# One activation table set with ln and exp, loaded by name, in the head of an S5 scan and MLP block

## The chip, the cores and the metric

The kernel runs on one core of a Trainium2 chip. The metric is the device time of one execution in microseconds (us). Before the change eight executions give a median of 165.45 us, from 165.26 to 919.03; all but the one of 919.03 lie between 165.26 and 165.62.

## The reference

The input x has 2048 rows of 448 features. Everything starts from a layer norm of x; a state space branch and an MLP branch read it, and the MLP branch norms it once more.

```python
xn = _layernorm(x)
# branch A: a complex diagonal recurrence over the 2048 rows
dt = exp(log_dt); Lam_bar = exp(dt * Lam)
B_bar = ((Lam_bar - 1) / Lam)[:, None] * Bmat
Bu = einsum("bld,pd->blp", xn, B_bar)
h_t = Lam_bar * h_{t-1} + Bu_t
s = 2 * einsum("blp,dp->bld", h, Cmat).real + xn * Dskip
# branch B: an MLP with 1792 hidden features
y = _layernorm(xn)
h = gelu(einsum("bsd,df->bsf", y, w1) + b1)
g = silu(einsum("bsf,fd->bsd", h, w2) + b2)
return x + s * g
```

## The kernel before

The 2048 rows are cut into four groups (`g`) of 512, each of two blocks (`b`) of 256 rows, and each block holds its even and odd rows apart (`par`, two halves of 128 rows on the partitions). The recurrence advances two rows at a time, so that a group has 256 steps (NK).

The kernel is written as a list of 603 tasks. Each names its engine, the keys it reads and writes, and one or more instructions. `emit` (L106) issues them in the order of a written-out list, `ORDER` (L146), and puts a semaphore wait ahead of an instruction where a key demands one; each engine works its own queue in that order. Some tasks have two forms, for VectorE or ScalarE, or for GpSimd or VectorE, and the list `SECOND` (L164) says which take the second. `ORDER` and `SECOND` come from a planner outside the file; the durations and priorities in the calls are what it was given, and the kernel itself doesn't use them.

The head of the program:

- `parameters` (L445): TensorE turns the parameter rows into columns; ScalarE copies them out of PSUM (L455, L456) and takes exp twice (L458, L466); GpSimd computes sines, cosines and the coefficients of B_bar and C on tiny tiles (L459 to L518).
- TensorE multiplies the identity by itself 28 times, and 8 times more after the parameters (L764).
- `first_norm` (L359) takes block 0 half by half: statistics (L366) and their aggregate (L367) on VectorE, 1/sqrt of the variance on ScalarE as ln (L368) and exp (L369), the scaling on VectorE (L371), four transposes on TensorE (L374), and the copy out of PSUM (L376). The last ln and exp there (L378) and two GpSimd operations (L380) give the scale of the first norm.
- Block 1 of group 0 is normed without ScalarE (L393 to L403, L416), and transposed by TensorE (L432, L438).

```python
kb.add("act", [lambda e, ...: e.activation(r1, var, ACT.Ln, scale=1.0 + LN_EPS, bias=eps[:, 1:2]),
               lambda e, ...: e.activation(r1, r1, ACT.Exp, scale=-0.5)], [f"mv0_{q}", "eps", "warm"], [f"r1{par}"],
       dur=0.5, lat=0.2, prio=4 * PINNED, chain=True, table="exp")
```

The program has no table loads written in it; they are put in when it is built, wherever the active set lacks the next function. L280 is an ln on one element early in ScalarE's queue.

Then the work on TensorE runs in one stream:

- `mm1_half` (L688): the first matmul of the MLP for group 0, one block at a time. Seven groups of eight matmuls for each block (L694), each into one of three pairs of PSUM banks, and a gelu out of PSUM (L701) by ScalarE for each. The first three groups read the first half of w1, the fourth both halves.
- `mm1` (L674): the same for a whole later group (L678, gelu L685).
- `mm2` (L705): the second matmul, 14 matmuls (L709), then the bias (L712), a tanh (L713) and the product (L714), which make silu.
- `bu` (L604): the input of the recurrence (L608), copied out by ScalarE (L612, L614); `ssm` (L622): rotations on VectorE (L625 to L629), the scans (L633), copies (L637, L638) and the rotation back into the states h_sb (L661 to L665).
- `ym` (L717): the output of the recurrence (L730, and L733 or L739), the product with the MLP's (L743), the residual (L745), and the store.
- `lb`, `cq`, `m0` (L567, L586, L594) build the weights of the recurrence from B and C: a scaling (L558 on ScalarE or L559 on VectorE), a multiply-add (L561), and products (L597). `tables` (L526) builds the rotation tables with ScalarE's sine (L545). `skips` (L519) builds diagonal matrices De and Do (L522 on ScalarE or L523 on VectorE).
- `ln_stats`, `ln_scale`, `ln_apply` (L348, L383, L409) norm a later group; the apply is L416 on VectorE or L417 on ScalarE. The transposes of normed rows (xnT, xn2T), of B (BT) and of C (Cr) go through SP's DMA queue (L83), as do nearly all loads (L84). The bias b2bc is loaded through GpSimd's queue.

Of the kernel before, what the change touches and what calls it, by code (L numbers as in the profile page):

```python
# [7 lines left out]
ACT = mybir.ActivationFunctionType  # L8
ALU = mybir.AluOpType
# [4 lines left out]
PINNED = -1e5  # L14
# [129 lines left out]


ORDER = [int(k) for k in """  # L146
11 13 18 22 12 10 0 19 23 1 9 20 24 5 81 21 25 16 17 14 27 2 3 6 26 15 83 28 4 84 29 89 8 36 85 30 38 90 86 82 91 7 31 87 39 92 41 32 40 42 88 46 95
93 43 33 47 45 94 48 34 96 97 106 57 98 44 108 49 107 99 100 35 101 55 110 50 56 109 51 112 111 37 141 102 114 113 103 138 144 104 136 52 177 134 58
142 116 115 60 59 61 105 143 53 118 179 65 150 54 117 165 62 120 151 63 119 163 64 148 69 137 122 149 66 121 152 67 146 124 68 155 123 70 71 153 126
76 156 125 77 75 154 128 79 166 127 80 73 157 130 140 72 145 74 299 78 147 132 129 298 131 272 303 300 178 133 304 301 181 305 302 139 306 135 158 164  # L150
268 273 167 180 169 159 168 160 170 182 280 173 161 307 183 310 316 308 317 174 309 313 311 229 269 171 312 314 276 172 230 185 175 162 176 184 231
270 186 274 271 358 277 232 318 275 278 281 233 279 282 315 359 283 360 188 234 237 187 235 361 238 362 190 236 239 189 246 364 363 247 191 243 319
242 193 365 366 194 195 245 320 196 368 197 402 367 406 403 321 407 404 369 408 405 370 409 322 240 410 241 248 323 244 371 199 200 257 372 324 203
251 411 252 414 253 412 254 417 204 255 256 198 420 258 325 259 373 415 260 376 261 418 326 201 416 202 215 421 216 380 205 219 377 220 378 206 249
384 379 413 223 217 224 374 227 250 207 385 218 386 462 375 208 387 221 228 209 463 222 225 464 226 210 381 263 382 466 465 383 262 211 467 264 468
328 212 265 192 266 470 327 267 469 329 213 471 336 333 472 214 509 513 506 474 510 473 334 337 284 508 475 512 507 511 335 514 476 285 286 330 331
338 287 477 347 515 518 348 349 332 519 480 350 351 288 340 341 342 289 343 516 290 344 339 345 346 291 481 478 353 482 479 517 488 292 293 520 483
352 294 354 489 484 355 490 356 419 295 357 491 296 422 554 485 297 521 388 522 524 555 486 423 389 525 390 487 391 424 425 392 393 395 426 427 396
397 398 428 523 432 429 399 558 526 430 400 431 394 433 556 401 559 438 437 527 557 434 435 442 562 528 436 451 439 444 452 529 453 441 454 563 455
440 560 443 445 446 447 448 449 530 566 450 456 561 457 531 567 458 459 564 532 460 461 536 533 565 535 492 537 534 544 568 545 493 494 540 538 495  # L160
539 542 546 572 496 548 543 497 541 499 573 547 569 570 576 550 574 500 498 571 501 549 580 551 552 553 502 575 581 577 582 587 503 578 583 504 584
579 505 588 589 591 585 586 590 595 592 593 599 596 594 597 600 598 601 602
""".split()]
SECOND = [int(k) for k in """  # L164
134 135 136 138 139 140 143 144 167 171 193 199 201 203 219 223 225 227 310 313 314 317 411 412 417 420 421 516 518 521 522 525
""".split()]


# [6 lines left out]
TWO_PI = 2.0 * math.pi  # L175


def bass_recurrent_scan__ssm_conv_s5__mixer_channel_mlp__prompt_kernel(
# [18 lines left out]
    with ExitStack() as es:  # L197
        def SB(name, shape, dtype=BF):
            return es.enter_context(nc.sbuf_tensor(name, shape, dtype))

        ident = SB("ident", [128, 128])
        mhalf = SB("mhalf", [128, 1, 1], F32)
        iota = SB("iota", [128, NK], F32)
        sgn = SB("sgn", [128, 4], F32)
# [54 lines left out]
        def pool(fn, reads=(), writes=(), dur=0.3, prio=0):  # L259
            kb.add("pool", fn, reads, writes, dur=dur, lat=0.15, prio=prio)  # L260

        def dve(fn, reads=(), writes=(), dur=0.2, prio=0):
            kb.add("dve", fn, reads, writes, dur=dur, lat=0.12, prio=prio)

        def act(fn, reads=(), writes=(), dur=0.6, prio=0, table=None):
            kb.add("act", fn, reads, writes, dur=dur, lat=0.2, prio=prio, table=table)

        def pe(fn, reads=(), writes=(), dur=0.2, prio=0):
            kb.add("pe", fn, reads, writes, dur=dur, lat=0.25, prio=prio)

        with nc.Block():

            S0 = -100
            pool(lambda e: e.memset(ident[:], 1.0), [], ["ident"], 0.2, S0)
            pool(lambda e: e.affine_select(ident[:], ident[:], [[1, 128]], ALU.is_equal, 0.0, base=0,
                                           channel_multiplier=-1), ["ident"], ["ident"], 0.4, S0)
            pool(lambda e: e.memset(sgn[:], -1.0), [], ["sgn"], 0.1, S0)
            pool(lambda e: e.affine_select(sgn[:, 0:1], sgn[:, 0:1], [[0, 1]], ALU.is_ge, 1.0, base=63,
                                           channel_multiplier=-1), ["sgn"], ["sgn"], 0.2, S0)
            act(lambda e: e.activation(sgn[0:1, 3:4], sgn[0:1, 2:3], ACT.Ln, scale=-1.0), ["sgn"], ["warm"], 0.2, 4 * PINNED, "exp")  # L280
            pool(lambda e: e.iota(iota[:], [[1, NK]], base=0, channel_multiplier=0,
                                  allow_small_or_imprecise_dtypes=True), [], ["iota"], 0.6, S0)

            pool(lambda e: e.tensor_scalar(sgn[:, 1:2], sgn[:, 0:1], -TWO_PI, None, op0=ALU.mult), ["sgn"], ["sgn1"], 0.2, S0)
            pool(lambda e: e.tensor_scalar(sgn[:, 2:3], sgn[:, 0:1], TWO_PI, None, op0=ALU.mult), ["sgn", "warm"], ["sgn2"], 0.2, S0)
            pool(lambda e: e.memset(sgn[:, 3:4], math.pi / 2), ["warm"], ["sgn3"], 0.1, S0)
            XN = ["xn0", "xn1"]
            XM = ["xm0", "xm1"]
            dve(lambda e: e.memset(vrows[:, 0:64], 0.0), [], ["vr"], 0.1, S0)
# [69 lines left out]
            def first_norm():  # L359

                for par in range(2):
                    q = 2 * par
                    var, mean = lnmv[:, 0, q, 1:2], lnmv[:, 0, q, 0:1]
                    r1 = lnw[:, 0, 2, 1, q:q + 1]
                    src, dst = x_all[:, 0, par, :], xn2_sb[:, 0, par * 512:par * 512 + D]
                    dve(lambda e, q=q, src=src: e.bn_stats(lnst[:, q, :], src), [f"x0p{par}"], [f"st{q}"], 0.62, 2 * PINNED + par)  # L366
                    dve(lambda e, q=q: e.bn_aggr(lnmv[:, 0, q, :], lnst[:, q, :]), [f"st{q}"], [f"mv0_{q}"], 0.16, 2 * PINNED + par)  # L367
                    kb.add("act", [lambda e, var=var, r1=r1: e.activation(r1, var, ACT.Ln, scale=1.0 + LN_EPS, bias=eps[:, 1:2]),  # L368
                                   lambda e, r1=r1: e.activation(r1, r1, ACT.Exp, scale=-0.5)], [f"mv0_{q}", "eps", "warm"], [f"r1{par}"],  # L369
                           dur=0.5, lat=0.2, prio=4 * PINNED, chain=True, table="exp")  # L370
                    dve(lambda e, src=src, dst=dst, mean=mean, r1=r1: e.tensor_scalar(dst, src, mean, r1, op0=ALU.subtract, op1=ALU.mult),  # L371
                        [f"x0p{par}", f"r1{par}", f"mv0_{q}", "xm0"], [f"xm0p{par}"], 0.4, 2 * PINNED + par + 0.5)
                    bank, oap = 6 - par, xn2T[:, 0, par * 4:par * 4 + 4, 0:128]
                    pe([lambda e, d=d, par=par, bank=bank: e.transpose(psh[:, bank, d * 128:(d + 1) * 128], xn2_sb[:, 0, par * 512 + d * 128:par * 512 + d * 128 + 128],  # L374
                                                                       ident[:, :]) for d in range(4)], [f"xm0p{par}", "ident"], [f"ps{bank}"], 0.33, 2 * PINNED)
                    dve(lambda e, bank=bank, oap=oap: e.tensor_copy(oap, psh[:, bank, 0:512].rearrange("p (d c) -> p d c", d=4)), [f"ps{bank}"], [f"xmT0p{par}"], 0.42, 2 * PINNED + 2)  # L376
                r0, n0, var = lnw[:, 0, 2, 0, 0:4:2], lnw[:, 0, 3, 0, 0:4:2], lnmv[:, 0, 0:4:2, 1]
                kb.add("act", [lambda e: e.activation(r0, var, ACT.Ln, bias=eps[:, 0:1]), lambda e: e.activation(r0, r0, ACT.Exp, scale=-0.5)],  # L378
                       ["mv0_0", "mv0_2", "eps", "r10", "r11"], ["r0"], dur=0.5, lat=0.2, prio=3 * PINNED, chain=True, table="exp")
                kb.add("pool", [lambda e: e.tensor_tensor(n0, lnmv[:, 0, 0:4:2, 0], r0, ALU.mult), lambda e: e.tensor_scalar(n0, n0, -1.0, None, op0=ALU.mult)],  # L380
                       ["mv0_0", "mv0_2", "r0"], ["lnw0_0"], dur=0.6, lat=0.15, prio=S0 + 2, chain=True)
# [467 lines left out]
```

## Time and profile before

| | |
|---|---|
| median of the runs | 165.45 us |
| the profiled execution's own time | 165.53 us |
| its span, from first to last instruction | 163.8 us |
| TensorE busy | 155.0 us, 95% of the span |
| VectorE busy | 124.6 us, 76% |
| ScalarE busy | 98.8 us, 60% |
| GpSimd busy | 33.8 us, 21% |
| mean granted clock of TensorE | 0.979 |
| chain that ended last, by engine | PE 91%, ACT 3%, DVE 2%, DMA 1%, issue 1% |

The profile is of one execution; its times are counted from the start of the span. PE is TensorE's matmul, PEld its weight load, DVE VectorE, ACT ScalarE, POOL GpSimd, and SP the engine that issues most transfers. A line such as L694 is a line of the kernel, and "a<-b" says what an operation writes and reads. The chain is followed back from the last instruction to whatever released it. A wait is written as the waiting operation, then the one that released it, then the total, the number and the longest.

### The profile page before, as it was taken

To read this page: it belongs to the slowest core of one execution; us is meant where nothing else is said; L and a number is where in the kernel's file an instruction comes from. 1 tells how busy PE (TensorE), PEld (TensorE's weight loads), DVE (VectorE), ACT (ScalarE), POOL (GpSimd) and SP (SyncE) were. 2 spreads that over 40 slices of the span, in tenths; PEclk is the share of its full clock that TensorE was granted. 3 is DMA by queue.
4 is the path that set the end of the run, shared out by engine and by line. 5 is a ranking of instruction groups with operands and counts; after the bars stand their busy time and mean duration, and the time that the engine had idled before them with its cause. 6 is when DMAs were issued, how large, how long until landed. Compare 5 with 4: busy or idle time off the path is not lost.

```text
span 163.8 us, 2747 instructions
## 1 busy us (share of the span) xinstructions
PE 155.0 (95%) x977; PEld 100.0 (61%) x977; DVE 124.6 (76%) x251; ACT 98.8 (60%) x156; POOL 33.8 (21%) x115
## 2 busy tenths in 40 slices
PE   5569999999999999999999999999999999999991
PEld 5448996567766765555555555566767675555560
DVE  5175698977498998899996969732499489987953
ACT  4998979987958599966544580452158953360200
POOL 5227795500000580000205420000002300000000
PEclk9956999999999999999999999999999999999999
DMA  4999946999874007300000056402060000010021
GB/s 100 332 284 382 255 58 139 185 161 179 164 147 116 0 0 133 107 0 4 0 0 0 2 123 122 112 0 56 4 168 0 0 4 0 0 56 0 35 83 58
DMA packets 29880, 14.61 MB, mean 89 GB/s; under 512 B 24581, under 2 KB 29577, under 8 KB 29866
## 3 DMA queue, kind: packets, MB, share of 16 engines
q1 hardware_dynamic: 29810, 14.31, 36.6%
q0 software_dynamic: 48, 0.11, 0.6%
q8 instruction: 8, 0.13, 0.3%
q14 instruction: 6, 0.05, 0.1%
q10 hardware_dynamic: 8, 0.00, 0.0%
HBM read 6.77 MB, written 1.84 MB: 53 GB/s over the span
## 4 chain that ended last, share of the span: by engine, by line
PE 91%; ACT 3%; DVE 2%; DMA 1%; issue 1%; DVEq 0%
PE psum L709 26%; PE psum L678 22%; PE psum L608 13%; PE psum L730 12%; PE psum L694 9%; PE psum L733 4%; PE psum L597 3%; ACT L369 2%; DMA x_all<-in_A_x_dram 1%; PE psum L739 1%; DVE t L743 1%; ACT L368 1%; DVE tmp L745 1%; DVE lnst L366 0%; PE psum L374 0%
## 5 line engine op out<-in xcount | busy, mean ns | idle before, releaser
L709 PE MATMUL psum<-w_sb,gT 128*128 128x448 bf16 x224 | 44.2, 352 | 0.0
L678 PE MATMUL psum<-xn2T,w_sb 128*128 128x512 bf16 x168 | 38.6, 379 | 0.0
L709 PEld LDWEIGHTS psum<-w_sb,gT 128*128 128x128 bf16 x224 | 21.8, 98 | 19.3
L685 ACT ACTIVATE gT<-psum 128x1024 bf16<-128x1024 f32 x21 | 21.5, 1024 | 14.9 <-PE psum L678 12.9
L678 PEld LDWEIGHTS psum<-xn2T,w_sb 128*128 128x128 bf16 x168 | 21.6, 132 | 12.5 <-issue 0.2
L608 PE MATMUL psum<-xnT,BT 128*128 128x256 bf16 x196 | 24.0, 273 | 0.0
L608 PEld LDWEIGHTS psum<-xnT,BT 128*128 128x128 bf16 x196 | 19.0, 98 | 4.7 <-ACT u_sb L612 0.3
L743 DVE TENSOR_TENSOR t<-psum,g_sb 128x448 bf16<-128x448 f32 (+2 forms) x17 | 10.1, 595 | 10.5 <-PE psum L733 8.5
L713 ACT ACTIVATE th<-o 128x448 f32<-128x448 f32 x16 | 8.8, 571 | 12.0 <-DVE o L712 11.9
L694 PE MATMUL psum<-xn2T,w_sb 128*128 128x256 bf16 x112 | 14.8, 301 | 0.6 <-issue 0.6
L633 DVE TENSOR_TENSOR_SCAN s_f<-cw,cur,v_sb 128x256 f32<-128x256 f32 x21 | 14.7, 736 | 0.3
L694 PEld LDWEIGHTS psum<-xn2T,w_sb 128*128 128x128 bf16 x112 | 13.2, 136 | 2.1 <-issue 0.8
L612 ACT ACTIVATE u_sb<-psum 128x512 bf16<-128x512 f32 x12 | 7.1, 595 | 10.0 <-PE psum L608 9.4
L712 DVE TENSOR_TENSOR o<-psum,b2bc 128x448 f32<-128x448 f32 x16 | 9.8, 622 | 4.4 <-PE psum L709 4.1
L730 PE MATMUL psum<-CQ,h_sb 128*128 128x448 bf16 (+2 forms) x63 | 12.0, 332 | 0.0
L730 PE MATMUL psum<-CZ,h_sb 128*128 128x448 bf16 x56 | 11.9, 352 | 0.0
L417 ACT ACTIVATE xn_sb<-x_all,lnw 128x448 bf16<-128x448 bf16 x16 | 11.4, 749 | 0.1
L714 DVE SCALAR_TENSOR_TENSOR g_sb<-th,o 128x448 bf16<-128x448 f32 x16 | 9.8, 619 | 1.9 <-ACT th L713 1.8
L701 ACT ACTIVATE gT<-psum 128x512 bf16<-128x512 f32 x14 | 8.2, 592 | 1.7 <-PE psum L694 1.5
L730 PEld LDWEIGHTS psum<-CQ,h_sb 128*128 128x128 bf16 x63 | 6.0, 98 | 4.2
L352 DVE BATCH_NORM_STATS2 lnst<-x_all 128x6 f32<-128x448 bf16 x14 | 8.3, 603 | 0.0
L730 PEld LDWEIGHTS psum<-CZ,h_sb 128*128 128x128 bf16 x56 | 5.4, 98 | 4.6
(151 smaller groups left out, 197.4 us busy)
## 6 DMA issues: line engine op xcount, KB each, us to landing
w_sb<-in_B_w_dram SPq DMA_DIRECT2D x2, 784.0 KB, 9.3
out_dram<-tmp SPq DMA_DIRECT2D x7, 224.0 KB, 2.2
w_sb<-in_B_w_dram SPq DMA_DIRECT2D x2, 672.0 KB, 6.2
x_all<-in_A_x_dram SPq DMA_DIRECT2D x3, 448.0 KB, 3.8
gT<-in_A_C_re_dram SPq DMA_DIRECT2D x1, 392.0 KB, 12.0
Bn<-in_A_B_re_dram SPq DMA_DIRECT2D x1, 336.0 KB, 8.2
Bn<-in_A_B_im_dram SPq DMA_DIRECT2D x1, 336.0 KB, 8.2
gT<-in_A_C_im_dram SPq DMA_DIRECT2D x1, 336.0 KB, 3.9
```

The costliest lines, as they stand in the source:

```text
L417: ("act", lambda e: e.activation(dst, src, ACT.Identity, bias=nb, scale=rs), 0.75, 0.2)]
L608: fns = [lambda e, r=r, m=m, d=d: e.matmul(psum[:, 4, r * NK:(r + 1) * NK], BT[:, m, d, :], xnT[:, gx, d, :], start=(d == 0), stop=(d == 6 ...
L633: dve(lambda e, i=i, ri=ri, init=init: e.tensor_tensor_scan(s_f[:, i, ri, :], col(R2, i).to_broadcast([128, NK]), v_sb[:, i, ri, :], init, ...
L678: fns = [lambda e, k=k, d=d: e.matmul(psum[:, b0 + k, :], w1_sb[:, d, fcol(2 * j + k)], rhs[:, d, :, :], start=(d == 0), stop=(d == 3)) fo ...
L685: act(lambda e: e.activation(gT[:, gb, 2 * j:2 * j + 2, :], psum[:, b0:b0 + 2, :], ACT.Gelu_apprx_tanh), [f"ps{b0}", f"ps{b0 + 1}"] + (WK ...
L694: fns = [lambda e, k=k, d=d: e.matmul(psum[:, banks[k], :].rearrange("p (r c) -> p r c", r=2)[:, :, cs], w1_sb[:, d, fcol(2 * j + k)], rhs ...
L709: fns = [lambda e, fi=fi: e.matmul(psum[:, bk, 0:D], gT[:, gb, fi, q * 128:(q + 1) * 128], w2_sb[:, fi, :], start=(fi == 0), stop=(fi == N ...
L712: dve(lambda e: e.tensor_tensor(o2[:, fb, :], psum[:, bk, 0:D], b2bc[:], ALU.add), [f"ps{bk}", "b2bc"], [f"oo{fb}"], 0.62, prio - 76)
L713: act(lambda e: e.activation(th[:, fb, :], o2[:, fb, :], ACT.Tanh, scale=0.5), [f"oo{fb}"] + (WK + WKP if g == 0 else []), [f"th{fb}"], 0. ...
L714: dve(lambda e: e.scalar_tensor_tensor(out=g_sb[:, gs, :], in0=th[:, fb, :], scalar=1.0, in1=o2[:, fb, :], op0=ALU.add, op1=ALU.mult), [f" ...
L730: fns = [lambda e, k=k: e.matmul(psum[:, bk, c0:c1], h_sb[:, hb, k, k0:k0 + 128], cm[:, k, c0:c1], start=(k == 0), stop=False) for k in ra ...
L743: dve(lambda e: e.tensor_tensor(t3[:, fb, c0:c1], psum[:, bk, c0:c1], g_sb[:, gs, c0:c1], ALU.mult), [f"ps{bk}", f"g{gs}"], [f"t3{fb}_{c0} ...
```

## The change

The activation of L280 is replaced by a load, by name, of the table set `natural_log_exp_and_others`, which waits for nothing. The keys that kept two small GpSimd operations (L285, L286) behind it go. The identity's two GpSimd operations get another priority. `ORDER` and `SECOND` are replaced whole.

```diff
 ORDER = [int(k) for k in """
-11 13 18 22 12 10 0 19 23 1 9 20 24 5 81 21 25 16 17 14 27 2 3 6 26 15 83 28 4 84 29 89 8 36 85 30 38 90 86 82 91 7 31 87 39 92 41 32 40 42 88 46 95
...
+0 11 18 22 12 1 10 19 23 13 9 81 20 24 2 14 3 21 16 25 6 7 27 17 15 5 26 83 8 28 4 84 29 89 38 85 30 90 82 86 91 31 87 39 92 32 41 40 42 88 46 95 93
...
 SECOND = [int(k) for k in """
-134 135 136 138 139 140 143 144 167 171 193 199 201 203 219 223 225 227 310 313 314 317 411 412 417 420 421 516 518 521 522 525
+135 137 138 142 143 163 165 167 173 175 201 203 215 221 223 225 227 310 313 411 414 418 420 421 515 516 522 524
...
-            pool(lambda e: e.memset(ident[:], 1.0), [], ["ident"], 0.2, S0)
+            pool(lambda e: e.memset(ident[:], 1.0), [], ["ident"], 0.2, 3 * PINNED)
             pool(lambda e: e.affine_select(ident[:], ident[:], [[1, 128]], ALU.is_equal, 0.0, base=0,
-                                           channel_multiplier=-1), ["ident"], ["ident"], 0.4, S0)
+                                           channel_multiplier=-1), ["ident"], ["ident"], 0.4, 3 * PINNED)
...
-            act(lambda e: e.activation(sgn[0:1, 3:4], sgn[0:1, 2:3], ACT.Ln, scale=-1.0), ["sgn"], ["warm"], 0.2, 4 * PINNED, "exp")
+            act(lambda e: e.preload_act_table_set("natural_log_exp_and_others"), [], ["warm"], 0.05, 5 * PINNED, "exp")
...
-            pool(lambda e: e.tensor_scalar(sgn[:, 2:3], sgn[:, 0:1], TWO_PI, None, op0=ALU.mult), ["sgn", "warm"], ["sgn2"], 0.2, S0)
-            pool(lambda e: e.memset(sgn[:, 3:4], math.pi / 2), ["warm"], ["sgn3"], 0.1, S0)
+            pool(lambda e: e.tensor_scalar(sgn[:, 2:3], sgn[:, 0:1], TWO_PI, None, op0=ALU.mult), ["sgn"], ["sgn2"], 0.2, S0)
+            pool(lambda e: e.memset(sgn[:, 3:4], math.pi / 2), ["sgn"], ["sgn3"], 0.1, S0)
...
-                           dur=0.5, lat=0.2, prio=4 * PINNED, chain=True, table="exp")
+                           dur=0.55, lat=0.2, prio=4 * PINNED, chain=True, table="exp")
```

What the new lists do on each engine's queue:

- GpSimd makes the identity ahead of the memset of M0 (L293), which was first. The load of b2bc, which stood behind L286, stands behind some 40 operations of the parameters.
- ScalarE's activations keep their order up to the second gelu. Later, among the tasks with two forms, it has 5 more of L558, 3 more of L522 and 3 fewer of L417; VectorE has 5 fewer of L559, 3 fewer of L523 and 3 more of L416.
- VectorE's first 23 rows (up to the apply of block 1 of group 0) are the same. Ahead of the last step of group 0's states (L665) it now has four statistics of group 3 (L352, L356), which stood behind it.
- TensorE's order is the same up to the first `mm2`. Then the group-1 `mm1` begins with two groups of eight and not one; the group-2 `mm1` begins ahead of the first `m0` and not behind it; the first `ym` comes behind five groups of group 2's `mm1` and not seven; one group of group 3's `mm1` goes earlier. The matmuls themselves are the same.
- SP's queue has the same loads up to x of group 1. Then C_im's larger piece is ahead of C_re, its last piece and two of the BT transposes are behind the transposes of group 1's xn2T and the first of its xnT, and later transposes of a group stand ahead of some of the stores.

## Prediction

> **What bounds the kernel now.** I read the waits of TensorE first, then the chain that ended last in order of time, then the stretches of TensorE's clock, then the landings of the loads. TensorE waits three times, and never after 10.39 us; from there to 158.6 us the chain is TensorE alone.
>
> ```profile
> PE psum L374 <- DVE xn_sb L371: 2.7, 1, 2.7
> PE psum L764 <- POOL ident L275: 1.8, 1, 1.8
> PE psum L694 <- issue: 0.6, 1, 0.6
> ```
>
> So the kernel is a head of 10.39 us, then 148.2 us of matmuls in a row, then 5.2 us of tail. The head is this part of the chain (start, length, what):
>
> ```profile
> 3.79 0.29 ACT lnw L368
> ...
> 4.11 1.28 ACT L369
> ...
> 5.40 0.20 ACT lnw L369
> ...
> 5.62 1.28 ACT L368
> ...
> 7.23 1.28 ACT L369
> 8.51 0.01 issue
> 8.52 0.21 ACT lnw L369
> 8.73 0.03 issue
> 8.76 0.41 DVE xn_sb L371
> 9.17 0.05 issue
> 9.21 0.61 PE psum L374 x4
> 9.82 0.56 issue
> 10.39 6.82 PE psum L694 x40
> ```
>
> The nameless ACT pieces of 1.28 us are table loads: the ln and the exp of each half of block 0 evict each other, and three loads lie between the first variance and the second half's scale. The first 40 matmuls take 6.82 us where the next 72 take 7.86 us, because of the clock (columns: stretch, its length, TensorE's busy time, and after POOL the granted clock):
>
> ```profile
> 4.85:8.27 3.42, 1.58 (x23) 1.08 (x21) 0.40 (x1) 3.36 (x5) 0.27 (x2) 1.00 1.02 320
> 8.27:11.68 3.41, 1.90 (x11) 1.33 (x12) 2.52 (x7) 3.32 (x8) 1.18 (x5) 0.50 1.03 273
> 11.68:15.10 3.42, 3.42 (x18) 2.47 (x17) 2.47 (x13) 3.21 (x7) 2.36 (x11) 0.50 1.07 365
> 15.10:18.50 3.40, 3.40 (x37) 3.39 (x36) 1.17 (x6) 2.96 (x6) 2.56 (x11) 1.00 1.06 359
> ```
>
> A stretch that is 46% busy is followed by half clock, one of 56% leaves it there, a full one lifts it. One limit lies just behind the head: the last piece of w1's second half, issued at 4.20 us, lands 7.7 us later, at 11.9.
>
> ```profile
> L84 SPq DMA_DIRECT2D w_sb<-in_B_w_dram x1: 497/497/497, 4.2 to 4.2; - x1
> ...
> DMA to landing us min/median/max: 7.7/7.7/7.7
> ```
>
> **What the skill says.** "ScalarE: Activation LUTs", Table sets: one named set, natural_log_exp_and_others, holds both functions; no run here shows that yet. The same page, What ACT_TABLE_LOAD costs: 1283 ns a load, equal for every set, and some 1380 ns of drain. The trace agrees on 1.28 us; the gaps around a load in the chain are 0.02 us, so I price a load at 1.3. "TensorE: Matmul & The Clock Gate", What's actually happening: the clock is decided in free-running windows of 3413 ns. The trace agrees: 8.27, 11.68 and 15.10 are 3.41 apart.
>
> **The change, part by part.** *Loads.* The order of the built program has one load ahead of the eight ln and exp activations instead of six, the other four (L701, L545, L713, L685) stay: 5 x 1.28 = 6.4 us less on ScalarE, plus the 0.20 us of L280's activation. What counts is the part ahead of TensorE. The one load now stands behind the ACT DMA issues (2.13 us) and ends at about 3.45, before the first variance at 3.77. Then ln and exp of half 0: 3.79 to 4.30. Half 1's variance ends at 4.30 + 0.18 = 4.48; its ln and exp (0.29 + 0.20) at 5.01; its L371 at 5.43 instead of 9.17. TensorE's four transposes of half 0 end at 6.49 as before (warm-up matmuls stand ahead), those of half 1 follow at once, to 6.8; the two copies L376 (0.42 each) run 6.53 to 7.37; matmuls follow 0.11 later, as before (10.28 to 10.39): 7.5. GpSimd now makes the identity before its 0.47 us memset, so TensorE's first warm-up moves 0.4 earlier and this may be 7.1; w1's first half, last piece issued at 2.18, lands 4.9 later, at 7.1, so not sooner.
>
> *What is late next.* Three groups of eight matmuls need only w1's first half; the fourth needs the second: 11.9. At full clock a matmul takes 7.86/72 = 0.11 us, at half 0.22. If the clock stays full, 24 take 2.6 and end near 10.1: TensorE stands for 1.8. If it drops at 8.27, seven are done by then and 17 x 0.22 = 3.7 end at 12.0. Either way group four begins at 12.0. Before: 22 matmuls by 15.10, two more by 15.3. Gain 15.3 - 12.0 = 3.3 us, not the 3.84 of three loads and not the 2.9 by which the start moves.
>
> *The clock after 12.0.* Not shown by the trace, bounded both ways. Stretch 4.85 to 8.27 will be some 70% busy (1.58, plus 0.77 to 1.1 of new matmuls), between 46 (dropped) and the 88 of the stretch before 4.85 (the warm-ups from 1.83 on, 0.11 us each; the eight after it take 0.08, so the clock was lifted). If it drops at 8.27 the next stretch is full and the clock is back at 11.68: cost nothing. If it stays, the next stretch is half busy; if that again suffices, cost nothing; if it drops at 11.68, then 14 matmuls run at half clock up to 15.10: 14 x 0.11 = 1.55 us. Two of three paths are free; I take nothing, range 0 to 1.55.
>
> *Evacuation.* The gelu load now ends near 8.0, before group one (8.4 at the soonest). 14 groups cost 0.59 each, and 2 L417 (0.75), 4 L522 (0.39), 2 L558 (0.65) go among them: 8.3 + 1.5 + 1.6 + 1.3 = 12.7 between 8.4 and 22.2; three pairs of banks give slack. Hidden; without that cover each L417 would cost 0.75.
>
> *b2bc.* Its DMA moves on GpSimd behind some 40 small operations, to about 18; at 7.3 us from issue to landing (as before, under more traffic) 25.3. Its first reader L712 comes at 24.9, the bank is wanted at 27.5: hidden, 0 to 0.4. Its 112 KB leave the first 12 us, which may bring w1 up to 0.4 us sooner.
>
> *The new order.* The matmuls are the same, so each wait is the question. I walked TensorE's new order with the old lengths (8 of L678 1.73, 14 of L608 1.53, 14 of L709 2.65, L730 1.32, L733 0.76), 3.3 ahead, and set against it when each operand is ready. Moved to DVE: 3 more L416 (0.39); moved to ScalarE: 5 L559 (0.45) and 3 L523 (0.25), so DVE loses 1.8 us net. Thin places: xn2T of group 1, wanted at 35.9; its last apply stands behind the sine table (load, five L545, one L417, to 30.2), the transpose goes out at 30.8 and takes 3.5 to 4.1: 34.9, slack 1.0. xn2T of group 2, now first used at 66.2 instead of 70.9: applies end at 61.3, lands 65.5, slack 0.7. States of group 0 (L665): ym now stands behind five mm1 groups of group 2, not seven: wanted at 87.33 - 3.3 - 2 x 1.73 = 80.6; DVE puts four more statistics (4 x 0.77) ahead of L665, but fewer L714 and L559; I get 78.2, slack 2.4. On SP's queue C_im's last piece and two BT transposes now go behind xn2T and xnT of group 1: the piece out at 34.7, landed 3.9 later at the latest, Cr's transposes (1.3 each) from 39.0 to 44.2, where they were 42.7 to 47.9; BT5 lands at 38.4, wanted at 39.4. I book 0.3 for all of it, range 0 to 2.
>
> *Sum.* Against the profiled execution: 165.53 (span 163.8, 1.73 around it) - 3.3 + 0.3 = 162.5; the median is 0.08 lower: 162.4.
>
> **Rivals.** (A) As above, 162.4. (B) The clock drops at 11.68 and takes back 1.55; TensorE is then later than its operands, so the 0.3 goes: 163.7. For it: 46 and 56% did not earn full clock. Against: two other paths. (C) The thin places give: 1 to 2 us of waits over A's, 163.9. For it: DVE is busy 34.5 of 37 us between 50 and 87. (D) Slower: the states of group 0 come late. If DVE gains nothing from the early head (it hangs on the Cr transposes) and pays all four statistics, L665 ends at 79.66 + 3.1 = 82.8; TensorE stands 2.2 of 3.41 us at L730, a stretch 35% busy, less than the 46% that cost the clock at 8.27, and a window at half clock adds 1.7: 162.1 + 3.9 = 166.0. It decides from L665 at about 82.6. Against: those transposes do come forward on SP's queue, and DVE has 1.8 less to do. (E) The set is not what it says, and loads come back: 165.5; the program's order has none.
>
> **Numbers.** A 0.50, B 0.27, C 0.13, D 0.07, E 0.03. Low end: w1 0.4 sooner and no wait, 161.7. High end: B with 0.6 of waits, 164.3. 0.2%, about what a measurement of this kernel can tell from no change, is 0.33 us: faster 0.90, same 0.03, slower 0.07.
>
> **What would show it.** One load at L280 and none at L368, L369, L378; L694 starting at 7.1 to 7.5; its 25th matmul at 12.0, behind w1; full clock from 11.68 (A) or 15.10 (B); no wait of TensorE over 0.5 us after 12. Wrong: a wait at L678 near 36 or 66, or at L730 near 80.

## The result, and the profile after

| | before | after |
|---|---|---|
| median of all runs | 165.44 us (31 runs) | 164.99 us (11 runs, 161.94 to 165.93) |
| the profiled execution: its time, its span | 165.53, 163.8 | 163.0, 161.3 |
| first L694, first L709, first L678 in the chain | 10.39, 25.52, 39.17 | 7.12, 20.40, 36.41 |

The ratio after to before is 0.9846, 95% interval 0.9821 to 0.9871, some 162.9 us; it leaves out runs more than 1.5% above the fastest of their kernel, and of the changed kernel's own eleven timed runs that is more than half, since they spread over 4 us where those of before lie within 0.9 (but for one at 919.03). So the change is a gain, about as large as forecast, that most executions don't get in full.

The profile of the changed kernel has one load ahead of ln and exp, and none between them (ScalarE's timeline; start, length, line and operation, and in brackets the idle time ahead and what ended it):

```profile
2.16 1.28 ACT L280 ACT_TABLE_LOAD   x1 [2.16 <-issue]
3.81 0.29 ACT L368 ACTIVATE lnw<-lnmv,eps 128x1 f32<-128x1 f32 x1 [0.37 <-DVE lnmv L367]
4.14 0.20 ACT L369 ACTIVATE lnw<-lnw 128x1 f32<-128x1 f32 x1
4.81 0.29 ACT L368 ACTIVATE lnw<-lnmv,eps 128x1 f32<-128x1 f32 x1 [0.46 <-DVE lnmv L367]
5.13 0.20 ACT L369 ACTIVATE lnw<-lnw 128x1 f32<-128x1 f32 x1
```

Before, 1.28 us of load stood between each pair; the named set does hold both functions, as the prediction took it. The waits of TensorE (the waiting operation, what released it, total, number, longest):

```profile
PE psum L678 <- DMA xn2T<-xn_sb: 1.4, 1, 1.4
PE psum L764 <- POOL ident L275: 1.4, 1, 1.4
PE psum L709 <- DVE o L712: 0.8, 1, 0.8
PE psum L694 <- DVE xn2T L376: 0.7, 1, 0.7
PE psum L694 <- issue: 0.2, 1, 0.2
```

The wait of 2.7 us at L374 is gone. Two are new and lie where TensorE never waited before: 0.8 us at L709 and 1.4 us at L678. The chain in order of time shows where:

```profile
7.12 2.80 PE psum L694 x24
9.92 0.24 issue
10.16 1.93 PE psum L694 x16
...
20.40 5.31 PE psum L709 x28
25.71 0.62 DVE o L712
26.33 0.14 issue
26.47 2.81 PE psum L709 x14
...
32.97 3.40 DMA xn2T<-xn_sb
36.37 0.05 issue
36.41 3.66 PE psum L678 x16
```

The first L709 comes 25.52 - 20.40 = 5.1 us earlier. From there to the first L678 it took 39.17 - 25.52 = 13.65 us before and takes 36.41 - 20.40 = 16.01 now: 2.36 us are given back, 0.8 and 1.4 of them in the two waits. After that little moves: 119.44 us from the first L678 to the last matmul's end before (158.61), 119.71 now (156.12). 5.12 - 2.36 - 0.27 = 2.49 us is the gain of this execution.

Two facts lie behind those numbers. The last piece of w1's second half, issued at 4.2 us as before, lands 5.9 us later, at 10.07, where it was 7.7 us. The fourth group of L694 starts there, at 10.16, though the profile names no releaser for it ("issue"):

```profile
L84 SPq DMA_DIRECT2D w_sb<-in_B_w_dram x2: 425/461/497, 3.7 to 4.2; - x2
...
DMA to landing us min/median/max: 5.8/5.8/5.9
```

And b2bc, whose turn on GpSimd came at 18.0, was issued at 21.91, after 3.9 us in which GpSimd did nothing (GpSimd's timeline):

```profile
17.79 0.22 POOL L490 TENSOR_SCALAR cw<-cw 128x4 f32<-128x4 f32 x1
21.91 0.80 POOL L84 DMA_DIRECT2D b2bc<-in_B_b_dram  x1 [3.91 <-issue]
```

It landed 3.8 us later, at 25.7, and there L712 starts (VectorE's timeline):

```profile
22.87 0.25 DVE L356 BATCH_NORM_AGGREGATE lnmv<-lnst 128x2 f32<-128x6 f32 x2
25.70 0.62 DVE L712 TENSOR_TENSOR o<-psum,b2bc 128x448 f32<-128x448 f32 x1 [2.58 <-PE psum L709]
```

The bracket names the matmuls, but the 14 that L712 needs were done by 23.05 (20.40 and 14 x 0.19): the one that came last was the load. Behind L712 in VectorE's queue stand the multiply-adds L561; the BT transposes on SP's queue wait for those, and xn2T of group 1 stands behind five BT transposes (SP's timeline):

```profile
21.07 10.50 SPq L83 DMA_TRANSPOSE BT<-Bn  x5
31.61 2.68 SPq L83 DMA_TRANSPOSE xn2T<-xn_sb  x2
```

### The profile page after: what moved, and what is told of

It reads as the page before. It is cut to its first block, busy times and chain, and to the rows that moved or that the text cites. A ratio compares the mean times of both kernels' runs of the same rounds, so it can differ in the third digit from the quotient of the medians.

```text
span 161.3 us, 2734 instructions
## 1 busy us (share of the span) xinstructions
PE 153.0 (95%) x977; PEld 99.0 (61%) x977; DVE 123.4 (77%) x246; ACT 95.0 (59%) x155; POOL 37.1 (23%) x115
## 4 chain that ended last, share of the span: by engine, by line
PE 91%; DVE 2%; DMA 2%; ACT 1%; issue 1%; POOL 0%; DVEq 0%; ACTq 0%; POOLq 0%
PE psum L709 25%; PE psum L678 23%; PE psum L608 12%; PE psum L730 12%; PE psum L694 8%; PE psum L733 4%; PE psum L597 3%; PE psum L764 2%; DMA xn2T<-xn_sb 2%; ACT tmp L558 1%; PE psum L739 1%; DVE t L743 1%; DVE tmp L745 1%; DVE xn2T L376 0%; DVE o L712 0%
## 5 line engine op out<-in xcount | busy, mean ns | idle before, releaser
L709 PE MATMUL psum<-w_sb,gT 128*128 128x448 bf16 x224 | 44.5, 352 | 0.8 <-DVE o L712 0.8
L678 PE MATMUL psum<-xn2T,w_sb 128*128 128x512 bf16 x168 | 39.1, 380 | 1.4 <-DMA xn2T<-xn_sb 1.4
L709 PEld LDWEIGHTS psum<-w_sb,gT 128*128 128x128 bf16 x224 | 21.7, 98 | 20.1 <-ACT WT L545 1.2
L678 PEld LDWEIGHTS psum<-xn2T,w_sb 128*128 128x128 bf16 x168 | 21.5, 132 | 14.1 <-DMA xn2T<-xn_sb 1.7
L712 DVE TENSOR_TENSOR o<-psum,b2bc 128x448 f32<-128x448 f32 x16 | 9.9, 622 | 6.8 <-PE psum L709 6.5
L694 PE MATMUL psum<-xn2T,w_sb 128*128 128x256 bf16 x112 | 12.8, 273 | 0.9 <-DVE xn2T L376 0.7
L694 PEld LDWEIGHTS psum<-xn2T,w_sb 128*128 128x128 bf16 x112 | 12.1, 132 | 1.3 <-DVE xn2T L376 0.9
L730 PE MATMUL psum<-CQ,h_sb 128*128 128x448 bf16 (+2 forms) x63 | 12.0, 332 | 0.0
L730 PE MATMUL psum<-CZ,h_sb 128*128 128x448 bf16 x56 | 11.9, 352 | 0.0
L417 ACT ACTIVATE xn_sb<-x_all,lnw 128x448 bf16<-128x448 bf16 x13 | 9.8, 753 | 2.1 <-DVE xn_sb L416 1.9
L701 ACT ACTIVATE gT<-psum 128x512 bf16<-128x512 f32 x14 | 8.2, 593 | 2.1 <-PE psum L694 1.8
L352 DVE BATCH_NORM_STATS2 lnst<-x_all 128x6 f32<-128x448 bf16 x14 | 8.3, 610 | 0.8 <-DMA x_all<-in_A_x_dram 0.8
L730 PEld LDWEIGHTS psum<-CQ,h_sb 128*128 128x128 bf16 x63 | 6.0, 98 | 4.4
L393 POOL TENSOR_SCALAR lnw<-lnmv 128x4 f32<-128x4 f32 x3 | 1.1, 380 | 32.1 <-DVE lnmv L356 32.0
```

Of the source, the lines that this page charges most:

```text
L417: ("act", lambda e: e.activation(dst, src, ACT.Identity, bias=nb, scale=rs), 0.75, 0.2)]
L678: fns = [lambda e, k=k, d=d: e.matmul(psum[:, b0 + k, :], w1_sb[:, d, fcol(2 * j + k)], rhs[:, d, :, :], start=(d == 0), stop=(d == 3)) fo ...
L694: fns = [lambda e, k=k, d=d: e.matmul(psum[:, banks[k], :].rearrange("p (r c) -> p r c", r=2)[:, :, cs], w1_sb[:, d, fcol(2 * j + k)], rhs ...
L709: fns = [lambda e, fi=fi: e.matmul(psum[:, bk, 0:D], gT[:, gb, fi, q * 128:(q + 1) * 128], w2_sb[:, fi, :], start=(fi == 0), stop=(fi == N ...
L712: dve(lambda e: e.tensor_tensor(o2[:, fb, :], psum[:, bk, 0:D], b2bc[:], ALU.add), [f"ps{bk}", "b2bc"], [f"oo{fb}"], 0.62, prio - 76)
L730: fns = [lambda e, k=k: e.matmul(psum[:, bk, c0:c1], h_sb[:, hb, k, k0:k0 + 128], cm[:, k, c0:c1], start=(k == 0), stop=False) for k in ra ...
```

## The experiments

My theory after the two traces: the loads are a gain of some 5 us because b2bc's traffic, gone from the first 12 us, lets w1 come sooner; 2.5 us of it are lost since b2bc comes too late at its new place. The rivals: the new order as a whole brings (or costs) the difference; or the spread is the clock's, and b2bc has no part in it. All ratios are against the kernel before. "Landing" below is that of w1's last piece after its issue at 4.2.

**b2bc through SP's queue.** The changed kernel with

```diff
-ld("pool", b2bc[:], dram_ap(B_b2, 0, [[0, 128], [1, D]]), ["b2bc"], 114688, -50, reads=["sgn3"])
+ld("sp", b2bc[:], dram_ap(B_b2, 0, [[0, 128], [1, D]]), ["b2bc"], 114688, -50)
...
+ORDER.remove(36); ORDER.insert(ORDER.index(37), 36)
```

> The changed kernel, with b2bc loaded through SP's queue just ahead of the load of x blocks 2 and 3, and not through GpSimd. Theory (GpSimd stood 3.9 us before it issued this load, so b2bc came 2.6 us late for L712, and what follows on VectorE and SP came late with it): L712 starts within 0.2 us of the end of its first 14 L709 matmuls (23.1), the TensorE waits of 0.8 us at L709 and 1.4 us at L678 go, and the time is 163.0 - 2.2 = 160.8 us, with runs that lie within 1 us of each other. Rival 1 (b2bc was not what L712 waited for, or x blocks 2 and 3 and the C matrices come later by as much): both waits stay within 0.5 us, 162.5 to 163.5. Rival 2 (the runs of the changed kernel at 165 us are another matter than b2bc): the profile is at 161, but the median stays above 163.5.

Measured: 162.14 us (161.41 to 163.56, 5 runs), 0.9789 (0.9768 to 0.9811). Below the changed kernel's interval, and rival 2 falls; but the theory's 160.8, with runs within 1 us, didn't come either. The profiled execution was this kernel's slowest, at 163.56, no faster than that of the changed kernel. The wait at L709 is gone there, but TensorE stood twice for w1 (its second half landed at 11.50), and 1.1 us at L678 stay, because this time x of blocks 2 and 3 was late (a wait of TensorE, then VectorE's timeline):

```profile
PE psum L694 <- DMA w_sb<-in_B_w_dram: 2.6, 2, 1.7
...
22.23 1.16 DVE L352 BATCH_NORM_STATS2 lnst<-x_all 128x6 f32<-128x448 bf16 x2 [2.15 <-DMA x_all<-in_A_x_dram]
```

They were there at 19.4 in the trace of the changed kernel. So L678 hangs on two things: the BT transposes ahead of xn2T, and x of blocks 2 and 3 behind w1, Bn, w2 and now b2bc on one queue.

**b2bc back at its early place on GpSimd**, the rest as changed:

```diff
+ORDER.remove(36); ORDER.insert(ORDER.index(8) + 1, 36)
```

> The changed kernel, with b2bc's load still on GpSimd but at its place of before, behind the memset L286, and so some 15 us earlier. Theory (the same as for b2bc on SP, and b2bc's early traffic is what kept w1's second half until 11.9 before): no wait at L712, no wait of 0.8 and 1.4 us, but w1's second half lands at 11.5 to 11.9 in place of 10.1, L694's 25th matmul goes then, and the time is 160.8 + 1.5 = 162.3 us. Rival (w1 came sooner for another reason, the earlier issue of loads on SP): w1 stays at 10.1 and the time is 160.8. If GpSimd's standing was not the cause of the late L712, it is 163 or above.

Measured: 164.66 us (163.12 to 167.04, 22 runs), 0.9916 (0.9895 to 0.9936). The waits at L709 and L678 went (0.2 left at L678), and w1 came late, more than expected: landing 9.3 us, at 13.5, with 3.1 us of TensorE standing ahead of it. By the ratios the early load costs more than the late one (0.9916 against 0.9846); the medians of all runs, 164.66 and 164.99, don't show it.

**The set alone.** The kernel before, in its own order:

```diff
-act(lambda e: e.activation(sgn[0:1, 3:4], sgn[0:1, 2:3], ACT.Ln, scale=-1.0), ["sgn"], ["warm"], 0.2, 4 * PINNED, "exp")
+act(lambda e: e.preload_act_table_set("natural_log_exp_and_others"), [], ["warm"], 0.05, 5 * PINNED, "exp")
```

with the two "warm" keys of L285 and L286 gone, as in the change.

> The kernel before in its own order, with nothing but the named set at L280 (and the two semaphore keys that go with it): one load in place of six. If the sum of the prediction holds for this part alone, L694 starts at 7.1 to 7.5, its 25th matmul waits for w1's second half at 11.5 to 12.0, and the time is 165.5 - 3.3 = 162.2 us with the full clock from 11.68. If the clock is lost in the window to 11.68, it is 163.7. If w1 comes sooner without the moved b2bc too, it is 161. If the loads were hidden, it is 165.4.

Measured: 164.0 us (163.09 to 166.64, 6 runs), 0.9893 (0.9871 to 0.9916). Nearer to 163.7 than to 162.2, for a reason that I had not put into any number: w1 came at 13.3, later than before (11.9), with b2bc issued at 3.5, ahead of both pieces of w1's second half (3.7 and 4.2), and not at 4.1 between them. In the profiled execution, one of the longer ones at 165.60, TensorE's waits have this line:

```profile
PE psum L694 <- DMA w_sb<-in_B_w_dram: 2.9, 1, 2.9
```

and the windows (columns as in the prediction) are these:

```profile
8.27:11.68 3.41, 2.23 (x21) 1.99 (x19) 1.47 (x5) 2.30 (x5) 2.37 (x11) 1.00 1.02 305
11.68:15.10 3.42, 1.68 (x8) 1.28 (x9) 3.04 (x16) 0.00 (x0) 2.59 (x13) 0.74 1.06 325
15.10:20.00 4.90, 4.90 (x43) 4.47 (x42) 2.87 (x9) 3.92 (x7) 3.36 (x16) 0.83 1.02 318
```

A w1 as late as this costs twice, here and in the trace with b2bc back at its early place: TensorE stands, and then goes on at half clock for a window, from 13.3 on here and from 13.1 there.

**The order alone.** The changed kernel with `preload_act_table_set("natural_log")` at L280, so that five loads come back.

> The changed kernel's order with six loads as before: L280 loads the set of ln alone, so that each exp and ln behind it loads its own again. If the loads and not the order bring the gain, L694 starts at 8.7 to 9.2, and b2bc's lateness costs as in the changed kernel: 163.0 + 1.6 = 164.6 us, or 166 and more if the clock drops in the window to 11.68 as before. If the new order brings most of the gain (w1 sooner at 10.1 in place of 11.9): 163.0 to 163.5.

Measured: 165.66 us (165.29 to 171.46, 22 runs), 1.0009 (1.0000 to 1.0019). No gain; L694 started at 10.49, not at 8.7 to 9.2, and b2bc's lateness costs nothing where everything else is late as well (issued at 23.8, after 0.55 us of standing, and read at 28.1).

**The set and b2bc on SP, in the old order**: the two edits above together, on the kernel before.

> The kernel before in its own order, with the named set at L280 and with b2bc loaded through SP's queue just ahead of the load of x blocks 2 and 3. Theory (the early b2bc load on GpSimd keeps w1's second half back: 11.3 to 13.4 us with it, 10.1 to 11.3 without it, in the five traces so far): w1's second half lands at 10.5 to 11.5 where it was 13.0 with the set alone, no lost clock, and the time is 164.0 - 2.0 = 162.0 us. Rival 1 (the new order is what gives the gain beside the loads): 163.5 to 164. Rival 2 (w1's landing is chance alone, whatever b2bc does): the runs spread from 163 to 166.6 as with the set alone.

Measured: 161.22 us (160.95 to 162.67, 6 runs), 0.9759 (0.9730 to 0.9788). All that the changed kernel was to bring, and without its order. w1 landed after 6.5 us, at 10.7; TensorE's waits are those of the head:

```profile
PE psum L764 <- POOL ident L275: 1.8, 1, 1.8
PE psum L694 <- ACT gT L701: 0.7, 1, 0.7
PE psum L694 <- DVE xn2T L376: 0.6, 1, 0.6
```

The second line names a gelu that the fourth group doesn't need: that group takes the first pair of banks again, and the gelu on that pair had ended at 8.97. What came last was w1, at 10.70, as the weight loads of the same matmuls say (TensorE's weight loads):

```profile
10.74 1.39 PEld L694 LDWEIGHTS psum<-xn2T,w_sb 128*128 128x128 bf16 x13 [0.91 <-DMA w_sb<-in_B_w_dram]
```

**C_im's larger piece late again**, on top of b2bc on SP in the new order (C_im's 336 KB behind the second BT transpose, its 56 KB piece in their early place):

```diff
+i, j = ORDER.index(178), ORDER.index(179); ORDER[i], ORDER[j] = 179, 178; ORDER.remove(178); ORDER.insert(ORDER.index(180) + 1, 178)
```

> The changed kernel with b2bc on SP, and with C_im's 336 KB piece put back to a late place on SP (behind the second BT transpose), its 56 KB piece in its stead, as the order before had it. Theory (C_im's 336 KB, moved into the early stretch by the new order, share the DMA engines with x blocks 2 and 3, whose landing at 22.2 in the trace with b2bc on SP set the end through xn2T): x blocks 2 and 3 land 1 us sooner or more, the wait of 1.1 us at L678 falls to 0.3 or less, and the time is 162.1 - 0.8 = 161.3 us. Rival (C's piece stands behind x in the queue and takes nothing from it): the same as with b2bc on SP, 162.1. If the later place holds up the BT transposes: 162.6 to 163.

Measured: 162.01 us (160.95 to 164.46, 6 runs), 0.9774 (0.9742 to 0.9807): the same as with b2bc on SP alone. x of blocks 2 and 3 came at 20.5 in this trace and at 22.2 in that, as the theory has it, but the medians don't differ: on the time the rival holds, and one landing from each kernel can't decide about C_im.

**Bn held back**, on top of b2bc on SP in the new order: the Bn loads wait for VectorE's second L371.

```diff
-        self.link()
+        self.link(); self.tasks[30].deps.add(self.tasks[92])
...
+ORDER.remove(31); ORDER.insert(ORDER.index(92) + 1, 31); ORDER.remove(30); ORDER.insert(ORDER.index(92) + 1, 30)
```

> The changed kernel with b2bc on SP, and with the Bn loads (784 KB, issued on SP right behind w1's second half) held until VectorE's second L371 is done, some 1.1 us later. Theory (w1's second half shares the DMA engines with what is issued behind it): it lands 0.5 to 1.0 us sooner, at 10 to 10.8, and the runs lie closer together; x blocks 2 and 3 and all behind them come up to 1 us later. If the start of L694's fourth group sets the end, the time is 162.1 - 0.6 = 161.5 us. If x blocks 2 and 3 do, through xn2T at L678: 162.5 to 163.

Measured: 161.23 us (160.68 to 163.78, 6 runs), 0.9758 (0.9722 to 0.9794). The runs lie no closer together. w1 landed after 5.9 us, at 10.08, as in the trace of the changed kernel, so these two compare well: L712 starts at 23.15 and not at 25.70, xn2T goes out 2.2 us sooner, and no wait is left at L709 or L678 (SP's timeline):

```profile
20.84 8.55 SPq L83 DMA_TRANSPOSE BT<-Bn  x5
29.44 2.68 SPq L83 DMA_TRANSPOSE xn2T<-xn_sb  x2
```

TensorE's waits there:

```profile
PE psum L764 <- POOL ident L275: 1.4, 1, 1.4
PE psum L694 <- DVE xn2T L376: 0.8, 1, 0.8
PE psum L694 <- ACT xn_sb L417: 0.4, 1, 0.4
```

(The last line is the fourth group again, which starts at 10.13, just behind w1.)

**b2bc on GpSimd, 5.5 us earlier**: `ORDER.remove(36); ORDER.insert(ORDER.index(51) + 1, 36)` in the changed kernel.

> The changed kernel with b2bc's load still on GpSimd, but some 5.5 us earlier in its order, behind the ten operations of the sine and cosine (12.4 us). Theory (GpSimd stands before it writes such a load while VectorE is busy without gaps): it stands 1 us or more here as well, since VectorE is busy from 13.1 to 19.1, but b2bc is there by 20 and L712 doesn't wait: the waits of 0.8 and 1.4 us fall, unless GpSimd's later steps come late by its standing, and the time is 162 to 163 us. Rival 1 (it stood for another reason, and does not here): it is issued at 12.4 to 12.8, and the time is as with b2bc on SP, 162.1. Rival 2 (the spread of the changed kernel has another cause): the median stays above 164 with no wait at L712.

Measured: 162.66 us (162.07 to 162.82, 4 runs), 0.9821 (0.9800 to 0.9842). It was issued at its turn, without standing, landed at 18.4, and L712 didn't wait for it (GpSimd's and VectorE's timeline):

```profile
12.99 0.82 POOL L84 DMA_DIRECT2D b2bc<-in_B_b_dram  x1
...
24.46 0.62 DVE L712 TENSOR_TENSOR o<-psum,b2bc 128x448 f32<-128x448 f32 x1 [0.46 <-PE psum L709]
```

The same queue, but in time: none of the four runs is above 162.82, where nine of the changed kernel's eleven are.

**A second load on GpSimd**: the kernel just told, and at the changed kernel's place a load of the same bytes into a tile that nobody reads.

```diff
+b2dummy = SB("b2dummy", [128, D])
...
+ld("pool", b2dummy[:], dram_ap(B_b2, 0, [[0, 128], [1, D]]), ["b2dummy"], 114688, -50)
...
+ORDER.insert(ORDER.index(36), 603)
```

> The kernel with b2bc on GpSimd behind the sine and cosine (162.66 us, no standing), and a second load of the same 112 KB into a tile that nobody reads, at the place on GpSimd where the changed kernel has b2bc. Nobody waits for its data, only GpSimd's own time is spent. If GpSimd stands there for 3 us or more again and this delays its steps at L393 to L397 and with them xn2T: a wait of 1 us or more at L678, 163.5 to 164.5 us. If it stands but only b2bc's late data cost anything: 162.5 to 163. If it doesn't stand (issued within 0.8 us of its turn), the 3.9 us of the changed kernel's one trace were a chance of that execution, or go with something else than the place: 162.7.

Measured: 161.65 us (160.75 to 163.46, 6 runs), 0.9762 (0.9726 to 0.9798). That is 1 us below the kernel without the second load, and nothing here explains it. GpSimd did not stand (GpSimd's timeline, no bracket):

```profile
19.86 0.22 POOL L490 TENSOR_SCALAR cw<-cw 128x4 f32<-128x4 f32 x1
20.03 0.61 POOL L84 DMA_DIRECT2D b2dummy<-in_B_b_dram  x1
```

I had thought of what the Trainium skill tells on "SBUF — State Buffer", SBUF: two separate sides: GpSimd writes the descriptors of its own DMAs, and can't while VectorE holds the port that they share. Here VectorE ran the same L561, L523 and L352 around 20.0 as in the changed kernel from 18.3 to 20.5, and GpSimd went at its turn; in the changed kernel it stood on through 0.23 us in which VectorE was idle (19.14 to 19.37). So these traces speak against that cause. What it was stays open.

**Bn held in the old order**, with the set and b2bc on SP.

> The order of before with the named set and b2bc on SP (161.22 us), and with the Bn loads held until VectorE's second L371 is done, as in the kernel that gave 161.23 with the new order. Theory (w1's second half, at 10.2 in the trace, no longer waits for the bytes of Bn; the old order costs nothing against the new): it lands at 9.6 to 10.1, and the time is 160.6 to 161.2 us, with no run above 162.5. If the start of the fourth group is set by the evacuations L701 (0.7 us in the trace) and no longer by w1: 161.2, as before. If Bn's lateness reaches the BT transposes and xn2T: 161.7 to 162.5.

Measured: 161.79 us (161.61 to 162.42, 5 runs), 0.9784 (0.9763 to 0.9804); landing 7.0 us, where it was 6.5 without the hold, and the fourth group starts with it (11.22 and 11.27). In the new order the landing went the other way, from 7.3 to 5.9. With one trace each that doesn't tell what Bn costs w1; in the times the hold brings no gain that can be told in either order (the intervals overlap).

**The kernel before with b2bc on SP**, all six loads kept.

> The kernel before with all its six loads and its own order, and only b2bc on SP, just ahead of x blocks 2 and 3. Theory (b2bc's early traffic costs only where w1's second half is waited for, and with six loads it isn't: group four went at 15.3, w1 was there at 11.9): 165.2 to 165.6 us, no change. If moving b2bc is a gain by itself, of the 2.8 us that it gave with the set: 162.7.

Measured: 165.67 us (165.30 to 166.23, 14 runs), 1.0010 (0.9998 to 1.0021): no gain, as the theory has it, though w1 landed after 6.5 us here. TensorE's timeline shows what stands ahead of it:

```profile
9.20 0.61 PE L374 MATMUL psum<-ident,xn_sb 128*128 128x128 bf16 x4 [2.19 <-DVE xn_sb L371]
10.33 3.41 PE L694 MATMUL psum<-xn2T,w_sb 128*128 128x256 bf16 x15 [0.52 <-DVE xn2T L376]
```

**w1's second half ahead of x block 1**, on top of Bn held in the old order: `ORDER.remove(28); ORDER.insert(ORDER.index(26), 28)` and the same for 29.

> The order of before with the named set, b2bc on SP, Bn held, and w1's second half issued on SP ahead of x block 1 (some 0.4 us sooner, x block 1 some 1 us later). If w1's second half still sets the fourth group: it lands 0.2 to 0.5 us sooner and the time is 0.2 to 0.4 us under the kernel with Bn held alone, 160.4 to 160.9. If x block 1 (its statistics, L352 and L432) is next: 0.5 us over it, 161.2 to 161.7.

Measured: 165.46 us (164.09 to 166.35, 14 runs), 0.9983 (0.9960 to 1.0007). Far worse than either expectation. w1 landed at 10.63, 0.6 us sooner, but x block 1 was issued 1.0 us later and landed 2.8 us later (4.31 + 6.7 = 11.0, where it was 3.32 + 4.9 = 8.2), and the norm of block 1 came too late for its transposes (TensorE's waits):

```profile
PE psum L432 <- DVE xn_sb L416: 2.8, 1, 2.8
```

All of the 3.7 us that the kernel with Bn held had gained was gone with one change of place. The trace with this wait is of one of the shorter runs, 164.17.

**What they settle.** Loads and b2bc can be set out as four corners, all in the old order:

| | six loads | the named set |
|---|---|---|
| b2bc on GpSimd, early | 165.44 us | 164.0, 0.9893 (0.9871 to 0.9916) |
| b2bc on SP, ahead of x blocks 2 and 3 | 165.67, 1.0010 (0.9998 to 1.0021) | 161.22, 0.9759 (0.9730 to 0.9788) |

The two are worth more together than apart: by the ratios, moving b2bc alone brings nothing, the set alone 1.8 us, both 4.0. The new order adds nothing that can be told: 165.66 with the loads back, and 162.14 against 161.22 with the set and b2bc on SP, intervals overlapping.

Landings of w1's last piece, one trace each, part by whether b2bc goes early on GpSimd: 7.7, 9.1 and 9.3 us where it does; 5.9, 5.9, 6.5, 6.5, 6.5, 6.7, 7.0, 7.1, 7.2 and 7.3 in the ten others with the same issue time. This is more than its bytes. The profile of the kernel before gives the load's packets (48 of them) 0.6% of 16 engines' span of 163.8 us, so some 1.0 us of every engine:

```profile
q0 software_dynamic: 48, 0.11, 0.6%
```

The Trainium skill, "DMA: Bandwidth & Descriptors", Queues, rings and completion order, says that each engine takes turns between the queues that it has work for, a packet at a time. That would fit: a load on GpSimd's queue pushes in between SP's, while on SP's own queue it waits behind w1. The runs show the outcome for b2bc, not the turns themselves, and 1.0 us is less than the 2.5 by which the middle landings part (9.1 and 6.6); the rest is open.

## Why the prediction was right or wrong

The direction and about the size were right: 162.4 forecast, 162.9 by the ratio, 163.0 for the profiled execution against a sum of 162.5. Yet the median of all runs, 164.99, lies above the range of 161.7 to 164.3, and that the sum came so near is luck: two wrong terms of opposite sign, the head (3.3 us for 5.1) and b2bc (at most 0.4 us for some 2.2).

- **Loads: right.** One load, at L280; L694 starts at 7.12, forecast 7.1 to 7.5. The gap between the load for L701 and the exp ahead of it is 0.02 us, so 1.3 for a load held.
- **What is late next: the mechanism right, a term mis-sized.** "Group four at 12.0" took w1's landing from the trace of before; the step on b2bc gave its leaving "up to 0.4 us". It was 1.8: group four began at 10.16. So the gain at the first L709 was 5.1 us and not 3.3. That the fourth group hangs on w1 was right: in nine of the eleven traces with the named set it starts within 0.1 us of w1's landing. Where b2bc does stay early, w1 is what is waited for, as forecast, but at 13.3 to 13.5.
- **The clock: case A in this trace**, at full pace from before 7.1 on. But the stretches that were priced, with ends at 8.27 and 11.68, were those of one execution. In this one the records of the clock begin at 5.60, so the windows of 3.41 us end at 9.01 and 12.43, and they were 79% and 93% busy. B's loss came in other kernels by another way, through w1: at 13.3 with the set alone, behind 2.9 us of standing.
- **Evacuation: hidden, as forecast.** The wait of 0.7 us that the profile puts down to L701, with the set and b2bc on SP, was for w1.
- **b2bc: the step that failed.** "Hidden, 0 to 0.4" priced it as landing by 25.3 against a reader at 24.9. It landed at 25.7, and the reader was ready at 23.05, since the head gained more. The cost was 2.2 us, shown by the kernel with Bn held (the same landing of w1, no late b2bc): in TensorE's timeline it took 14.0 us from the start of L709 to that of L678 (20.2 to 34.2), the changed kernel 16.2 (20.2 to 36.4). That 25.3 lies so near 25.7 is luck: 18 + 7.3 was forecast, 21.9 + 3.8 measured. Had GpSimd gone at its turn, 18.0 + 3.8 = 21.8 (an estimate from this trace) would have been in time: the standing was not in my range at all.
- **The new order: the right place, the wrong reason.** xn2T of group 1 was "wanted at 35.9, there 34.9". It was wanted at 35.0 and there at 36.4, through L712, L561 and BT, a chain that I had not drawn; for b2bc I had asked only when TensorE wants its bank. The sign that the prediction named as "wrong", a wait at L678 near 36, came: rival C has its wait, not its cause. The other thin places, L678 near 66 and L730 near 80, showed no wait.
- **The spread was not foreseen at all.** Three things were seen to differ between executions: when w1's second half lands, when b2bc lands, and when TensorE comes to full pace (below). The changed kernel's runs at 165 to 166 us go with b2bc's place: of the three kernels that move only b2bc, the two with it on SP or 5.5 us earlier on GpSimd have no run above 163.56 in nine; the third, with it early, has such runs again, and a late w1 in its trace. What happens in those runs, a longer standing or something else, no trace shows.
- Rivals D and E didn't occur.

The best versions, 161.22 (the set and b2bc on SP in the old order), 161.23 and 161.65, can't be told apart; the first is the smallest edit.

## What to carry to other kernels

When a change takes a stall out of the head, ask again of every load that the stall had covered when it lands, who is on its queue and who pushes in from another: here the place of a load of 112 KB was worth 2.2 of 4.0 us. A load that "has plenty of time" did best here on the queue of what is waited for, and behind it. When a profile names a releaser that had long been done, look for a landing at that moment: at the fourth group, and at L712, it was a load each time. And with several loads in a near race, one trace is one draw: price the landing with a range taken from more than one, and read the spread of the runs as well as the median.

## What was not expected of the hardware

- GpSimd stood 3.9 us ahead of one DMA, with nothing in the trace to wait for. In two other traces it stood 0.55 us, or not at all, ahead of a load of the same bytes at the same place in its order.
- A clock that reads 1.00 need not mean full pace. In the kernel before with b2bc on SP, 15 matmuls of L694 take 3.41 us from 10.33 on (the line above), 0.23 each, against 2.80 / 24 = 0.12 in the changed kernel, and yet the stretch reads 1.00:

```profile
11.68:15.10 3.42, 3.42 (x23) 2.79 (x22) 2.49 (x12) 3.34 (x8) 2.31 (x11) 1.00 1.06 395
```

  The trace holds no record of the clock before 13.9 us there, and a stretch without one reads as 1.00. The records begin where the pitch of the matmuls changes: at 13.9 there, at 10.5 with the second GpSimd load, at 5.6 in the changed kernel. The Trainium skill, "TensorE: Matmul & The Clock Gate", What's actually happening, says that the windows run free of the kernel's start, so that the moment differs by execution; these traces agree. It also follows that a run's mean clock doesn't tell how long its head went at half pace: of 43 runs of the kernel before, those at 0.979 have a median of 165.50 us (15 runs), those at 1.000 one of 165.58 (8 runs).
- A stand of TensorE of some 3 us cost the clock in two traces and not in a third. With the set alone TensorE was busy for 0.61 us of the window from 9.89 to 13.31, with b2bc early on GpSimd for 0.73 us of that from 9.69 to 13.10, and a window at half clock followed. With w1's second half ahead of x block 1, the stand of 2.8 us fell into two windows, busy for 2.13 us (10.50 to 13.91) and 1.90 us (13.91 to 17.33), and the clock stayed full. The ends of the windows are those of the clock's records, and steps of 3.41 us from them.
